# Two orders changed in the weight and attention prologue: w2's tiles go between the blocks of w3 @ w_out, and the last early pair makes its x before what the next pair needs

## The chip, the cores and the metric

The kernel runs on one core of one Trainium2 chip. The metric is device time in microseconds (us) of one execution. Three executions of the kernel before took 998.71, 1000.65 and 995.85 us; their median is 998.71 us. A further execution was profiled; it took 999.64 us, and its span from the first to the last instruction is 997.8 us.

## The reference

Block-causal attention over 8 batches of 8 heads (576 positions, head dimension 64), whose output is the input x of a gated MLP without a nonlinearity. In short:

```python
scores = scale * q @ k.T            # masked: a block of 64 sees itself and earlier blocks
attn   = exp(scores - max) ; attn /= attn.sum(-1) + 1e-9
x      = (attn @ v)                 # 4608 tokens x 512
out    = ((x @ w1) * (x @ w2) @ w3) @ w_out
```

## The kernel before, in words

Attention goes by pairs of heads: pair n holds heads 2(n mod 4) and 2(n mod 4)+1 of batch n div 4, 32 pairs in all, four pairs to a batch. Within a pair, j = 0, 1 is the head. The MLP goes by batch and by half of the tokens. Products are of float32r halves: a value is kept as a high part (`w1h`, `xh`) and the small rest (`w1l`, `xl`), and three products stand for one.

There are two phases. In the **early phase** (pairs 0 to 3, the whole of batch 0) the weights are made ready beside the attention. The weights come from memory as int64 views of doubles; `load_w` (L122) fetches one tile of 512 KB (`wraw`, five buffers) through the SP queue, ACT takes an absolute value (L137), and DVE puts the bits together in three operations (L138, L139, L142). For tiles of w1 and w2 `load_split` (L146) adds an ACT cast to the high part (L148) and a DVE subtraction for the rest (L149). w3 and w_out are multiplied together first: eight blocks `w` of eight products each (L359), copied out on ACT (L347) and DVE (L348) into `wh` and `wl`. The generator `gen_w` (L337) sets that order: 8 tiles of w_out, then for each of the 8 blocks two tiles of w3 and one tile of w1 (`rows1`), and behind them the 8 tiles of w2: 40 steps, one for each letter C of the plan.

A pair is written out by a string of letters, one string for each j. S is a tile of scores (`s_tile`, L223: two products for each part, then the exponentials on ACT). V is a step of scores @ v (tile `x`, L270 early, L286 late). M is a step of `shift_mask` for the **next** pair (L162): bf16 casts `kb` and `qd` on ACT, six groups of products `mx` (L180), their maxima `m` on DVE (L184, L186), a transpose on PE (`mt`, L188), a scaled copy on ACT (`ms`, L190), and two small transfers that put the row into `qk` of each j (L197). A and B are the halves of q and k for the next pair's j = 0 and this pair's j = 1 (L205, L207, L208). N takes `x` out of PSUM (`tr`, L310; L312), T divides by the sums and makes `xh` and `xl` (`norm` L320, `finish_x` L326). Q prepares v and loads the raw q, k and v of the pair after next (L94).

In the early phase a scheduler orders each engine's instructions once, when the program is built; all steps but C have the higher priority there. From pair 4 on (the **late phase**) PE's order is the written one: the scores of pair 4 (`s`, L231) come first, then the first products of the MLP (`ab`, L382), which read `xh` and `xl` of all four pairs of batch 0. Each engine works its list in order. The early tiles and the late tiles share memory.

The names and lines that matter below: `ms` and `qk` (L190, L197), `s` (L231), `x`, `rr`, `rb`, `xh`, `xl` (L310 to L334), `wraw`, `wbits`, `w2h`, `w2l` (L132 to L149), `kb`, `qd` (L158), `mx`, `m`, `mt` (L180 to L188), `ab` (L382). In the changed kernel the same statements stand 7 or 8 lines lower (`s` is L238 there, `ab` L390).

Of the kernel before, what the change touches and what calls it, by code (L numbers as in the profile page):

```python
# [17 lines left out]
B, H, S, D = 8, 8, 576, 64  # L18
BLK = 64
NB = S // BLK  # L20
NPAIR = H // 2
# [3 lines left out]
NC = DM // P  # L25
# [17 lines left out]
PLAN = (  # L43
    "B F B F S F S B F F S S F F F S M M V F V V V F R F F V Q N",
    "M A S S A F F S F M M S F F F S M A M V V V F V F F V N Q F R T M F F",
)

EARLY_PLAN = (
    "M S S S C S C C C C M S V V B C M M V A V M V M Q B M A B M N",
    "S C C S A S S C S C V V V V V Q N T",  # L50
)

DELAY = 3
# [5 lines left out]
def block_causal_attention__then__gated_mlp_kernel(ctx, tc, qkv, consts, ident_in, w1, w2, w3t, wout, out_t):  # L59
    nc = tc.nc  # L60
    w1, w2, w3t, wout = (w.bitcast(I32) for w in (w1, w2, w3t, wout))
# [12 lines left out]
    w1h = cpool.tile([P, NC, DF], F32R, name="w1h")  # L74
    w1l = cpool.tile([P, NC, DF], F32R, name="w1l")
# [7 lines left out]
    w2h = cpool.tile([P, NC, DF], F32R, name="w2h")  # L83
    w2l = cpool.tile([P, NC, DF], F32R, name="w2l")
# [37 lines left out]
    def load_w(dst, src, k):  # L122

        t = tl["early"].tile([P, 1024], F32, tag="wraw", name="wraw", bufs=5)
        u = tl["early"].tile([P, 512], F32, tag="wbits", name="wbits", bufs=6)  # L130
        wide = t.bitcast(I32)
        nc.sync.dma_start(out=wide.rearrange("p (k w) -> p k w", k=k), in_=src)  # L132
        wide = wide.rearrange("p (c two) -> p c two", two=2)
        low, high = wide[:, :, 0], wide[:, :, 1]
        bits = u.bitcast(I32)
        V = nc.vector
        nc.scalar.activation(u, high.bitcast(F32), AF.Abs, scale=2.0**-112)  # L137
        V.tensor_scalar(out=bits, in0=bits, scalar1=3, scalar2=0x7FFFFFF8, op0=ALU.logical_shift_left, op1=ALU.bitwise_and)  # L138
        V.scalar_tensor_tensor(out=bits, in0=high, scalar=-0x80000000, in1=bits, op0=ALU.bitwise_and, op1=ALU.bitwise_or)  # L139
        if dst is None:  # L140
            dst = u.unsqueeze(1)
        V.scalar_tensor_tensor(out=dst.bitcast(I32), in0=low.rearrange("p (k w) -> p k w", k=k), scalar=29,  # L142
                               in1=bits.rearrange("p (k w) -> p k w", k=k), op0=ALU.logical_shift_right, op1=ALU.bitwise_or)
        return u

    def load_split(dst_h, dst_l, src):  # L146
        val = load_w(None, src.unsqueeze(1), 1)
        nc.scalar.copy(dst_h, val)  # L148
        nc.vector.tensor_tensor(out=dst_l, in0=val, in1=dst_h, op=ALU.subtract)  # L149

    def load_rows(dst_h, dst_l, src, c):
        for h in range(2):
            cs = slice(h * 512, (h + 1) * 512)
            load_split(dst_h[:, c, cs], dst_l[:, c, cs], src[c * P : (c + 1) * P, h * 1024 : (h + 1) * 1024])
            yield
# [43 lines left out]
    def prep_qk(n, j):  # L199
        rqk = raw_of[n][:, 0 : 2 * S].rearrange("p (t s) -> p t s", t=2)  # L200
        o, x = own[j], oth[j]
        if j == 1:
            shift(n, 1)
        high, low = qk[j][o, 0::3, :], qk[j][o, 1:3, :]
        cast(n, high, rqk[o], CAST[0])  # L205
        yield
        nc.sync.dma_start(out=qk[j][x, 0::2, :].bitcast(F32), in_=high.bitcast(F32))  # L207
        (nc.vector if n <= EARLY else nc.gpsimd).tensor_tensor(out=low, in0=rqk[o], in1=high, op=ALU.subtract)  # L208
        yield
# [86 lines left out]
    def sums(n, j, part):  # L296

        blocks = tl["sum"].rearrange("p (b c) -> p b c", c=32)
        nc.vector.tensor_reduce(part[:, j, :], blocks, axis=AX.X, op=ALU.add, apply_transpose=True)
# [7 lines left out]
    def take_early(n, j, xps, x32, rr):  # L307
        o, x = own[j], oth[j]
        tr = work.tile([P, S], F32, tag="tr", name=f"tr{n}_{j}")
        nc.vector.transpose(tr[o], xps[x, 384:960])  # L310
        nc.vector.tensor_scalar_add(rr[o], tr[o].rearrange("p (b c) -> p b c", c=32)[:, :, 0], 1e-9)
        nc.scalar.copy(x32[o], xps[o, 384:960])  # L312
# [24 lines left out]
    def gen_w(wp):  # L337
        wo = tl["wo"]
        for k in range(NF):
            load_w(wo[:, k : k + 1, :], wout[k * P : (k + 1) * P, :].unsqueeze(1), 1)  # L340
            yield
        rows1 = (None for c in range(NC) for _ in load_rows(w1h, w1l, w1, c))
        pending = []

        def evacuate():
            m, acc = pending.pop(0)
            nc.scalar.copy(wh[:, m, :], acc)  # L347
            nc.vector.tensor_tensor(out=wl[:, m, :], in0=acc, in1=wh[:, m, :], op=ALU.subtract)  # L348

        for m in range(NF):  # L350
            t3 = wp.tile([P, NF, P], F32, tag="w3", name="w3", bufs=2)
            for k in range(0, NF, 4):
                src = w3t[k * P : (k + 4) * P, 2 * m * P : 2 * (m + 1) * P].rearrange("(k p) f -> p k f", p=P)
                load_w(t3[:, k : k + 4, :], src, 4)
                if k == 0:
                    yield
            acc = ps_m.tile([P, 512], F32, tag="psm", name=f"w{m}")
            for k in range(NF):
                nc.tensor.matmul(acc, t3[:, k, :], wo[:, k, :], start=(k == 0), stop=(k == NF - 1))  # L359
            pending.append((m, acc))  # L360
            if len(pending) > 1:
                evacuate()
            yield
            next(rows1)
            yield
        while pending:
            evacuate()
        for c in range(NC):
            yield from load_rows(w2h, w2l, w2, c)

    def gen_moe(b):
        mp, gh, gl = tl["late"], tl["gh"], tl["gl"]
# [33 lines left out]
    def fill(g, k):  # L406
        for _ in range(k):
            if next(g, "end") == "end":
                return
# [7 lines left out]
    for j in range(2):  # L417
        prep_v(0, j)
    load(1)
    weights = gen_w(wp)  # L420

    def pair(n):

        early = n < EARLY
        x32 = work.tile([P, S], F32, tag="x32", name=f"x32_{n}")
        rr = work.tile([P, S // 32], F32, tag="rr", name=f"rr{n}")
        part = None if early else work.tile([P, 2, S // 32], F32, tag="part", name=f"part{n}")
        last = n + 1 == NN
        masks = iter(()) if last else shift_mask(n + 1)
        own_qk = prep_qk(n, 1)  # L430
        next_qk = iter(()) if last else prep_qk(n + 1, 0)
        for j in range(2):
            xps = ps_x.tile([P, 1024], F32, tag="psx", name=f"x{n}_{j}")
            p_early = wp.tile([P, 1600], F32, tag="pe", name=f"pe{n}_{j}") if early else None
            tiles = iter(S_TILES)
            pvs = (pv_early if early else pv)(n, j, xps, p_early)
            delay = DELAY if n == NPAIR and j == 0 else 0
            for step in (EARLY_PLAN if early else PLAN)[j].split():
                if step == "C":
                    fill(weights, 1)  # L440
                    continue
                with tc.high_priority(offset=0) if early else nullcontext():
                    if step == "S":
                        s_tile(n, j, next(tiles), p_early)
                    elif step == "F":
                        if delay:
                            delay -= 1
                        else:
                            fill(mlp, 1)
                    elif step == "M":  # L450
                        fill(masks, 1)
                    elif step == "A":
                        fill(next_qk, 1)
                    elif step == "B":
                        fill(own_qk, 1)
                    elif step == "V":
                        fill(pvs, 1)
                    elif step == "R":
                        sums(n, j, part)
                    elif step == "N" and early:  # L460
                        take_early(n, j, xps, x32, rr)
                    elif step == "N":
                        take(n, j, xps, x32)
                    elif step == "T":
                        if not early:
                            total(n, part, rr)
                        norm(n, x32, rr)
                        finish_x(n, x32)
                    elif step == "Q" and not last:
                        if n + 1 != NPAIR:  # L470
                            prep_v(n + 1, j)
                        if j == 1 and n + 2 < NN:
                            load(n + 2)
# [64 lines left out]
```

## Time and profile before

| | |
|---|---|
| three runs, us | 998.71, 1000.65, 995.85 |
| median, us | 998.71 |
| profiled execution: time / span, us | 999.64 / 997.8 |
| instructions in the trace | 18149 |
| busy share of the span: PE, DVE, ACT, POOL | 96%, 71%, 55%, 52% |
| mean granted TensorE clock | 0.989 |

Shares over the whole span mix three stages: the early phase (to about 148 us), the late phase with attention and MLP together (to about 950 us), and the last MLP alone. The page's 40 slices show DVE at 7 to 9 tenths in the first six slices and PE at 9 tenths from then on; the slices of POOL are 0 up to there. So the rows further down are by stage: busy time of each engine in a stretch, who waited for whom in it, and the single instructions around the hand-over from the early to the late phase.

### The profile page before, as it was taken

Reading aid. Unit: us, or ns where it says so; the run is one execution under the profiler, and the core shown is the slowest. Engines: PE = TensorE matmul, PEld = TensorE weight load, DVE = VectorE, ACT = ScalarE, POOL = GpSimd, SP = SyncE. Lnnn points to the kernel's source line nnn. Section 1 sums busy time; section 2 is a strip of 40 time slices with the busy share of each in tenths; the row PEclk is TensorE's granted clock in tenths of the full one; section 3 lists DMA queues with packets and bytes.
Section 4 is the critical chain, followed back from the end, with each engine's and each line's share of the span. In section 5 each row is a group of like instructions: output and inputs, shape, how many; then the busy total and the mean of one; then the engine's idle time right before and its main releaser. Section 6 shows DMA issues by size and latency. Waiting matters only on the chain.

```text
span 997.8 us, 18149 instructions
## 1 busy us (share of the span) xinstructions
PE 959.7 (96%) x6624; PEld 884.9 (89%) x6624; DVE 705.7 (71%) x1316; ACT 546.5 (55%) x1433; POOL 520.3 (52%) x525
## 2 busy tenths in 40 slices
PE   3799979999999999999999999999999999999998
PEld 2455459999999999999999999999999999999998
DVE  7889987777777777777777777777777777774100
ACT  4556765555555656555556556555555555554221
POOL 0000007666666657676666756666665757573211
PEclk9799989999999999999999999999999999999999
DMA  7777521221222122212212221221221222100000
GB/s 235 232 254 239 184 94 35 64 73 56 79 62 86 58 77 62 64 47 74 72 57 79 62 86 50 86 61 47 64 74 62 68 79 62 45 17 26 3 23 24
DMA packets 36409, 80.39 MB, mean 81 GB/s; under 512 B 4384, under 2 KB 20896, under 8 KB 36320
## 3 DMA queue, kind: packets, MB, share of 16 engines
q1 hardware_dynamic: 36320, 79.23, 26.5%
q8 instruction: 52, 0.85, 0.4%
q14 instruction: 37, 0.30, 0.1%
HBM read 50.76 MB, written 9.44 MB: 60 GB/s over the span
## 4 chain that ended last, share of the span: by engine, by line
PE 69%; DVE 17%; ACT 7%; issue 4%; DMA 2%; DVEq 0%; ACTq 0%; SPq 0%
PE ab L382 28%; PE o L398 21%; PE s L231 7%; DVE pl L249 6%; PE x L286 5%; PE mx L180 3%; PE w L359 3%; ACT p L246 2%; DVE g L389 2%; ACT ph L247 2%; PE x L270 2%; DVE m L184 1%; DMA wraw<-in_w 1%; DVE x L324 1%; ACT a L387 1%
## 5 line engine op out<-in xcount | busy, mean ns | idle before, releaser
L252 POOL TENSOR_TENSOR rsum<-rsum,p 128x448 f32<-128x448 f32 x224 | 177.9, 794 | 120.7 <-ACT p L246 114.0
L249 DVE TENSOR_TENSOR pl<-p,ph 128x448 fp32r<-128x448 f32 x168 | 150.8, 911 | 65.0 <-ACT ph L247 64.2
L390 ACT CAST gh<-g 128x288 fp32r<-128x288 f32 x128 | 55.4, 433 | 218.1 <-DVE g L389 218.1
L391 POOL TENSOR_TENSOR gl<-g,gh 128x288 fp32r<-128x288 f32 x128 | 108.2, 845 | 122.6 <-ACT gh L390 122.5
L231 PE MATMUL s<-qk 128*128 128x288 f32 (+4 forms) x768 | 159.5, 315 | 5.0 <-DMA qk<-ms 2.2
L382 PE MATMUL ab<-xh,w1h 128*128 128x288 f32 x512 | 151.9, 297 | 3.5 <-ACT xh L333 3.5
L382 PE MATMUL ab<-xh,w2h 128*128 128x288 f32 x512 | 153.9, 301 | 0.0
L398 PE MATMUL o<-gh,wh 128*128 128x288 f32 x512 | 153.5, 300 | 0.0
L382 PE MATMUL ab<-xl,w1h 128*128 128x288 f32 x512 | 151.6, 296 | 0.0
L382 PE MATMUL ab<-xh,w1l 128*128 128x288 f32 x512 | 151.6, 296 | 0.0
L382 PE MATMUL ab<-xl,w2h 128*128 128x288 f32 x512 | 151.1, 295 | 0.0
L382 PE MATMUL ab<-xh,w2l 128*128 128x288 f32 x512 | 151.1, 295 | 0.0
L398 PE MATMUL o<-gh,wl 128*128 128x288 f32 x512 | 150.9, 295 | 0.0
L398 PE MATMUL o<-gl,wh 128*128 128x288 f32 x512 | 150.9, 295 | 0.0
L208 POOL TENSOR_TENSOR qk<-raw,qk 64x1152 fp32r<-64x1152 f32 x54 | 144.2, 2671 | 2.0
L184 DVE TENSOR_REDUCE m<-mx 128x1 f32<-128x512 f32 (+6 forms) x320 | 128.6, 449 | 20.7 <-PE mx L180 18.9
L221 POOL TENSOR_TENSOR vs<-raw,vs 128x320 fp32r<-128x320 f32 x56 | 49.6, 887 | 166.5 <-ACT vs L158 166.5
L231 PEld LDWEIGHTS s<-qk 128*128 128x128 f32 (+1 forms) x768 | 116.8, 184 | 19.1 <-issue 7.0
L247 ACT ACTIVATE ph<-s 128x288 fp32r<-128x288 f32 x336 | 131.3, 393 | 0.0
L246 ACT ACTIVATE p<-s 128x448 f32<-128x448 f32 x224 | 85.4, 381 | 45.3 <-PE s L231 44.2
L389 DVE TENSOR_TENSOR g<-ab,a 128x288 f32<-128x288 f32 x128 | 57.7, 451 | 73.6 <-PE ab L382 70.4
L286 PE MATMUL x<-ph,vs 128*128 128x128 f32 x336 | 104.1, 319 | 0.0
(70 smaller groups left out, 2134.1 us busy)
## 6 DMA issues: line engine op xcount, KB each, us to landing
raw<-in_qkv SPq DMA_DIRECT2D x32, 896.0 KB
qk<-qk SPq DMA_DIRECT2D x64, 288.0 KB
out_t<-o SPq DMA_DIRECT2D x64, 144.0 KB
wraw<-in_w3t SPq DMA_DIRECT2D x16, 512.0 KB
wraw<-in_w SPq DMA_DIRECT2D x16, 512.0 KB
wraw<-in_wout SPq DMA_DIRECT2D x8, 512.0 KB
qk<-ms SPq DMA_DIRECT2D x64, 2.2 KB
cst<-in_consts SPq DMA_DIRECT2D x1, 288.0 KB
```

Source lines behind the costliest of these rows:

```text
L184: nc.vector.reduce_max(m[:, col : col + 1], sc, axis=AX.X)
L208: (nc.vector if n <= EARLY else nc.gpsimd).tensor_tensor(out=low, in0=rqk[o], in1=high, op=ALU.subtract)
L231: nc.tensor.matmul(t[ks, at : at + q1 - q0], qk[j][:, 2 + s, kr], qk[j][:, s, q0:q1], start=(s == 0), stop=(s == 1))
L246: nc.scalar.activation(p32, t[ks, at : at + w], AF.Exp, scale=SCALE)
L247: nc.scalar.activation(ph[ks, o : o + w], t[ks, at : at + w], AF.Exp, scale=SCALE)
L249: nc.vector.tensor_tensor(out=low, in0=p32, in1=ph[ks, o : o + w], op=ALU.subtract)
L252: nc.gpsimd.tensor_tensor(out=r, in0=r, in1=p32, op=ALU.add)
L286: nc.tensor.matmul(xps[:, to : to + w], v[:, c, :], pr[:, a : a + w], start=(u < 2 and s == 0), stop=(u in (0, len(PV) - 1) and s == len(p ...
L382: nc.tensor.matmul(t[:, 0:HALF], l[:, c, fs], r, start=(c == 0 and s == 0), stop=(c == NC - 1 and s == 2))
L389: nc.vector.tensor_tensor(out=g32, in0=acc[1][:, 0:HALF], in1=a32, op=ALU.mult)
L391: nc.gpsimd.tensor_tensor(out=gl[:, f, :], in0=g32, in1=gh[:, f, :], op=ALU.subtract)
L398: nc.tensor.matmul(t[:, 0:HALF], l[:, f, es], r[:, f, :], start=(f == 0 and s == 0), stop=(f == NF - 1 and s == 2))
```

## The change

Two things change. In `gen_w` one list of tiles holds w1's eight and then w2's eight, and `ROWS` says how many of them follow each block of w3 @ w_out: 1, 1, 2, 2, 2, 2, 2, 2. Fourteen go between the blocks, and two remain for the end. In the last early pair (pair 3) the plan is `LAST_PLAN`: no M and no A before the T that finishes x; then nine M and four A, which belong to pair 4. The first three early pairs keep their plan.

```diff
+ROWS = (1, 1, 2, 2, 2, 2, 2, 2)
+
+LAST_PLAN = (
+    "S S S S C C S V V B B V V V Q C C C C C N",
+    "S S S S S V V V V V C C C C C N T Q M M M M M M M M M A A A A",
+)
...
-        rows1 = (None for c in range(NC) for _ in load_rows(w1h, w1l, w1, c))
+        rows = (None for d in ((w1h, w1l, w1), (w2h, w2l, w2)) for c in range(NC) for _ in load_rows(*d, c))
...
-            next(rows1)
-            yield
+            for _ in range(ROWS[m]):
+                next(rows)
+                yield
         while pending:
             evacuate()
-        for c in range(NC):
-            yield from load_rows(w2h, w2l, w2, c)
+        for _ in rows:
+            yield
...
-            for step in (EARLY_PLAN if early else PLAN)[j].split():
+            for step in (PLAN if not early else LAST_PLAN if n + 1 == NPAIR else EARLY_PLAN)[j].split():
```

On DVE, the end of the early phase before. `tr`, `rr`, `rb`, `x_3` and `xl` are pair 3's x; `m_932` is the maxima for pair 4, `qk_85` its q and k of j = 1, `pl` pair 4's exponentials.

```order
L186 TENSOR_REDUCE m_932<-m_932 128x1
L139 SCALAR_TENSOR_TENSOR wbits<-wraw,wbits 128x512
L138 TENSOR_SCALAR wbits<-wbits 128x512
...
L310 STREAM_TRANSPOSE tr_1_1067<-x_1_998 64x576
...
L208 TENSOR_TENSOR qk_85<-raw_834,qk_85 64x1152
L149 TENSOR_TENSOR w2l<-wbits,w2h 128x512
...
L324 TENSOR_TENSOR x_3_852<-x_3_852,rb_1072 128x576
L249 TENSOR_TENSOR pl<-rsum,ph 128x288 x2
L334 TENSOR_TENSOR xl_0_1076<-x_3_852,xh_0_1075 128x288
L334 TENSOR_TENSOR xl_1_1080<-x_3_852,xh_1_1079 128x288
```

The same place on DVE now (`m_1047` are the maxima for pair 4):

```order
L156 TENSOR_TENSOR w2l<-wbits,w2h 128x512
L317 STREAM_TRANSPOSE tr_1_1025<-x_1_965 64x576
L191 TENSOR_REDUCE m_1047<-mx_0_1048 128x1
...
L331 TENSOR_TENSOR x_3_845<-x_3_845,rb_1030 128x576
L191 TENSOR_REDUCE m_1047<-mx_4_1064 128x1
L191 TENSOR_REDUCE m_1047<-mx_2_1054 128x1
L191 TENSOR_REDUCE m_1047<-mx_4_1064 128x1
L341 TENSOR_TENSOR xl_0_1034<-x_3_845,xh_0_1033 128x288
L191 TENSOR_REDUCE m_1047<-mx_5_1069 128x1 x2
L341 TENSOR_TENSOR xl_1_1038<-x_3_845,xh_1_1037 128x288
L193 TENSOR_REDUCE m_1047<-m_1047 128x1
L215 TENSOR_TENSOR qk_85<-raw_827,qk_85 64x1152
L256 TENSOR_TENSOR pl<-rsum,ph 128x288 x2
```

The last tile of w2 and the whole of x now stand before the last maximum of pair 4; before, the maxima were done first, and x came last.

On PE, the hand-over before: the scores' first product, the transpose of the maxima, the other scores, and the MLP.

```order
L270 MATMUL x_1_998<-pe_1_999,ve_144 128x64
L231 MATMUL s_0_1108<-qk_84 128x288
L188 MATMUL mt_989<-ident,m_932 9x128
L231 MATMUL s_0_1108<-qk_84 128x288
L231 MATMUL s_0_1114<-qk_84 128x288 x2
L382 MATMUL ab<-xh_0_353,w1h 128x288
```

And now:

```order
L277 MATMUL x_1_965<-pe_1_966,ve_144 128x64
L238 MATMUL s_0_1108<-qk_84 128x288
L187 LDWEIGHTS qd
L187 MATMUL mx_3_1059<-kb_1043,qd 128x384
...
L187 LDWEIGHTS qd
L187 MATMUL mx_5_1069<-kb_1043,qd 128x64
L195 MATMUL mt_1075<-ident,m_1047 9x128
L238 MATMUL s_0_1108<-qk_84 128x288
L238 MATMUL s_0_1114<-qk_84 128x288 x2
L390 MATMUL ab<-xh_0_353,w1h 128x288
```

Groups 3 to 5 of `mx` moved behind the last product of pair 3's x; the order from `mt` on is as it was.

On SP, the transfers at the end of the early phase before (`raw_1065` is pair 5's q, k and v):

```order
L132 DMA wraw<-in_w 128x1024 x2
L197 DMA qk_85<-ms_752 1x9x64
L207 DMA qk_85<-qk_85 64x2x576
L132 DMA wraw<-in_w 128x1024
L94 DMA raw_1065<-in_qkv 128x1792
L207 DMA qk_84<-qk_84 64x2x576
```

And now (`raw_1041` is the same data):

```order
L139 DMA wraw<-in_w3t 128x4x256 x2
L139 DMA wraw<-in_w 128x1024
L101 DMA raw_1041<-in_qkv 128x1792
L139 DMA wraw<-in_w 128x1024 x3
L214 DMA qk_84<-qk_84 64x2x576
```

The raw load of pair 5 moved ahead of the last three tiles of w2.

## Rows read from the trace of the kernel before

**Rows 1.** Stretches: length, busy us of each engine, clock, DMA share, GB/s

```profile
65.00:148.00 83.00, 74.12 (x265) 41.77 (x264) 80.63 (x156) 55.73 (x112) 2.37 (x2) 0.97 0.59 186
148.00:950.00 802.00, 797.12 (x5902) 775.53 (x5902) 570.53 (x1058) 448.76 (x1237) 509.61 (x508) 1.00 0.21 61
```

**Rows 2.** PE in order of time: start, us, instruction [idle before]

```profile
135.20 0.52 PE L180 MATMUL mx<-kb,qd 128*128 128x320 bf16 x4
...
137.94 0.27 PE L188 MATMUL mt<-ident,m 128*9 128x128 f32 x1
140.41 1.09 PE L231 MATMUL s<-qk 128*128 128x288 f32 x3 [2.19 <-DMA qk<-ms]
141.29 0.44 PE L382 MATMUL ab<-xh,w1h 128*128 128x288 f32 x1
...
143.21 0.44 PE L382 MATMUL ab<-xl,w1h 128*128 128x288 f32 x1
147.11 0.61 PE L382 MATMUL ab<-xh,w1h 128*128 128x288 f32 x1 [3.46 <-ACT xh L333]
...
148.10 1.48 PE L231 MATMUL s<-qk 128*128 128x448 f32 x4
```

**Rows 3.** DVE's waits, 65 to 148 us

```profile
DVE tr L310 <- PE x L270: 0.7, 1, 0.7
```

**Rows 4.** DVE in order of time

```profile
52.89 0.69 DVE L184 TENSOR_REDUCE m<-mx 128x1 f32<-128x512 f32 x1 [2.23 <-PE mx L180]
...
135.73 1.22 DVE L184 TENSOR_REDUCE m<-mx 128x1 f32<-128x320 f32 x4 [0.57 <-PE mx L180]
...
137.59 0.15 DVE L186 TENSOR_REDUCE m<-m 128x1 f32<-128x2 f32 x1
137.66 0.68 DVE L139 SCALAR_TENSOR_TENSOR wbits<-wraw,wbits 128x512 int32<-128x512 int32 x1
138.26 0.42 DVE L138 TENSOR_SCALAR wbits<-wbits 128x512 int32<-128x512 int32 x1
138.59 0.69 DVE L142 SCALAR_TENSOR_TENSOR wbits<-wraw,wbits 128x512 int32<-128x512 int32 x1
...
139.91 0.78 DVE L310 STREAM_TRANSPOSE tr<-x 64x576 f32<-64x576 f32 x1
...
142.14 1.35 DVE L208 TENSOR_TENSOR qk<-raw,qk 64x1152 fp32r<-64x1152 f32 x1
...
146.46 0.82 DVE L249 TENSOR_TENSOR pl<-rsum,ph 128x288 fp32r<-128x288 f32 x2
147.19 0.82 DVE L334 TENSOR_TENSOR xl<-x,xh 128x288 fp32r<-128x288 f32 x2
```

**Rows 5.** ACT in order of time

```profile
135.76 0.67 ACT L158 CAST kb<-raw 128x576 bf16<-128x576 f32 x1 [0.18 <-PE mx L180]
136.34 0.61 ACT L148 CAST w2h<-wbits 128x512 fp32r<-128x512 f32 x1
136.86 1.35 ACT L158 CAST qd<-raw 64x576 bf16<-64x576 f32 x2
138.25 0.27 ACT L190 ACTIVATE ms<-mt 9x128 fp32r<-9x128 f32 x1
```

**Rows 6.** Stretches of the hand-over, columns as in Rows 1

```profile
140.00:143.60 3.60, 3.19 (x12) 2.90 (x12) 3.51 (x6) 2.16 (x5) 0.49 (x1) 0.53 0.01 1
...
147.10:150.30 3.20, 3.19 (x11) 3.02 (x12) 1.11 (x4) 1.90 (x6) 0.59 (x1) 0.50 0.62 255
```

**Rows 7.** SP's issues: start, us; the second a late w2 tile's

```profile
95.25 7.94 SPq L132 DMA_DIRECT2D wraw<-in_w  x5
...
118.33 0.52 SPq L132 DMA_DIRECT2D wraw<-in_w  x1
```

**Rows 8.** That late tile's first use, on ACT

```profile
122.47 0.67 ACT L137 ACTIVATE wbits<-wraw 128x512 f32<-128x512 f32 x1 [0.18 <-DMA wraw<-in_w]
```

**Rows 9.** Chain that ended last: start, us, one transfer of a w tile

```profile
96.78 6.12 DMA wraw<-in_w
```

## The prediction

> **What bounds the kernel now.** I read the busy time of each engine by stretches first [rows 1]. From 148 to 950 us PE is busy for 797.12 of 802.00 us at full clock: whatever the early phase ends late or early by is handed through to the end, since there is no slack of PE in which it could be caught up. From 65 to 148 us it is DVE that is full, 80.63 of 83.00 us; PE's 74.12 there are products waiting in its pipeline. So the question is when the early phase hands over. Next I read PE's instructions around the hand-over in order of time, with what ended each idle stretch [rows 2]. Two waits count: 2.19 us of the scores `s` for the row of maxima that a transfer puts into `qk`, and 3.46 us of `ab` for `xh`, pair 3's x. The reader is to see that PE has finished `mt` at 138.21 and stands until 140.41, does three products of `s` and nine of `ab` to 143.65, stands until 147.11, and then never again: at 148.10 come the next scores, and the late phase runs. The second wait is the one that the new order of pair 3 takes away, for x is then finished before the masks of pair 4. What it puts last instead is the row of maxima.
>
> **The first part, w2's tiles earlier.** On DVE no instruction is added or taken away; the early list holds the same operations in another order. Up to about 69 us the list is also in the same order. From there to the hand-over DVE had no more than two real waits, 0.7 us for `x` [rows 3] and 0.57 for `mx` [rows 4], 1.3 us together. A better order can save at most these, a worse one can add some; the longest wait that DVE had for another engine earlier is 2.23 us [rows 4]. Both ends kept, I take half of the 1.3 as saved, 0.65 us. w2 ready earlier is worth nothing by itself: its first use is behind `s` and twelve `ab`. `wh` and `wl`, now ready later, are wanted only by the second MLP stage. Both are covered by the work of the late phase.
>
> **The second part, x first, step by step.** *When DVE is through.* Before, its last early work, `xl`, ends at 147.19 + 0.82 = 148.01; the two `pl` between 146.46 and 147.19 belong to pair 4 and take 0.73 [rows 4]. Without them the early work ends at 147.28, with 0.65 saved at 146.6. In the new order the last early operation is `qk_85` (L215), so 146.6 is its end; the bounds are 146.0 (1.3 saved) and 148.8 (2.23 added).
>
> *When the row of maxima is there.* Counted back from that end: `qk_85` 1.35, the small reduction 0.07 from start to start, two `xl` of 0.37 each, and the maxima of 192, 256 and 64 columns. Four maxima of 832 columns in all went in 1.22 [rows 4], so these 512 columns are some 0.7. That makes 2.85: at 143.75 the PSUM buffer of the last mask group comes free. Its two products follow, some 0.4 (four took 0.52 [rows 2]), to 144.15. Then ACT: `ms` stands behind `kb` and both `qd` of pair 5, which may start only when those products have read `kb` and `qd`. Before, `kb` started at 135.76 and `ms` at 138.25, with one `w2h` of 0.52 from start to start between them that is not there any more [rows 5]: 2.49 - 0.52 = 1.97. So `ms` starts at 146.1. (By the other way, through the last reduction and `mt`, it could start at 146.6 - 1.35 + 0.5 = 145.75, where 0.5 is from the end of L186 to `ms` [rows 4, 5]; ACT's casts are later and decide.) From the start of `ms` to the first `s` after the transfer it was 140.41 - 138.25 = 2.16 [rows 2, 5]. So PE starts at 146.1 + 2.16 = 148.3. Behind that wait on PE stands everything: the other scores and all of `ab`, though x is ready some 3 us earlier. That is what is late next.
>
> *What PE then has to do.* Before, it had done three `s` and nine `ab` while x was on its way, and had three `ab` left. Now three `s` and all twelve `ab` lie between the wait and the next scores. At the low clock three `s` took 0.88 and one `ab` 0.24 ((143.21 - 141.29) / 8) [rows 2]: 0.88 + 2.88 = 3.76. The next scores would be at 152.1, against 148.10.
>
> *The clock.* After its wait for x, PE ran at 0.50 of full clock, level 1.2 GHz, from 147.1 to 150.3, and at full clock in the stage that follows; behind the first wait it was 0.53 over 3.6 us [rows 1, 6]. In the new order there is one long stand, and before it PE has only masks and the rest of x. I take the same 3.2 us of low clock, 148.3 to 151.5. Then the last 0.56 us of the 3.76 take half, and the next scores start at 151.8: 3.7 us later than before. At that point the kernel before still had 2.2 us of low clock ahead, which cost it 1.1; the new one has none. Sum: 3.7 - 1.1 = 2.6 us slower. The bounds: with 146.0 and full clock at once the 3.76 shrink to 1.88, the point comes at 149.6, and the sum is 149.6 - 148.1 - 1.1 = 0.4; with 148.8 and a low clock as long as both stretches of before together, 6.8 us, it is 2.6 + 2.2 + 1.8 = 6.6. I take 2.6, since both stands of before were followed by a low clock of about that length.
>
> The Trainium skill, page "TensorE: Matmul & The Clock Gate", section "HAM oscillation — how this bites in real kernels", says that a pause in the products is paid twice, once as the pause and again as throttled products after it. Rows 6 show that here behind both pauses. By that rule the sum is 2.6; without it, with full clock at once, it would be 3.76 / 2 + 148.3 - 148.1 - 1.1 = 1.0.
>
> Against the profiled execution that is 999.64 + 2.6 = 1002.2 us. That execution lay 0.93 over the median of the three runs; by the median it is 998.71 + 2.6 = 1001.3 us, which I forecast.
>
> **Rivals.** *The gain is what it looks like.* If the row of maxima were there before PE needs it, the 3.46 us of wait for x and the low clock behind it (3.2 / 2 = 1.6) would go: 999.64 - 5.1 = 994.5, by the median 993.6. For it speaks that the wait for x is the longest of PE at the hand-over [rows 2]. Against it stands the order: no `ab` comes before the second `s`, and the last maximum is the last but one of DVE's early operations. Chance 0.05.
>
> *Even.* The new wait is as long as the old, with full clock soon behind it: the sum of the lower bound, 0.4, to 1.0: 999.1 to 999.7 by the median. For it speaks that the maxima wait and the x wait hang on the same full DVE. Chance 0.22.
>
> *A wait on the last w2 tile, slower.* On SP the raw load of pair 5 now stands before the last three tiles. The last tile may be asked for when the fifth tile before it has been read, and between that and its own first DVE operation stand ten operations of DVE: six of 0.60 from start to start, two of 0.33, a transpose of 0.78 [rows 4] and a small one of some 0.1, 5.1 us, less 0.67 for ACT's step [rows 8]: 4.4 us for the transfer. A tile of the end of the phase took 122.47 - 118.33 = 4.14 [rows 7, 8], and fits; one of five that were issued from 95.25 on took 6.12 [rows 7, 9], and DVE would stand 1.7 us. From 4.4 us of transfer on this decides; with it nothing of DVE's 1.3 is saved either, and the sum is 2.6 + 1.7 + 0.65 = 5.0, by the median 1003.7 and more if two tiles are late. Chance 0.25 for this and all else that is over 5 us.
>
> The Trainium skill, page "DMA: Bandwidth & Descriptors", section "Anatomy of one DMA — SWDGE (gpsimd) path", gives a transfer as 2.0 us and a share by size; for 512 KB that is 3.2 us, an estimate by that page for another issuing path. Rows 7 and 8 show 4.14, and the measurement decides. By the page the last tile would have 1.2 us to spare, and this rival would fall.
>
> *The change doesn't do what it says* is excluded by the order: x does come before the maxima, w2 before the last block.
>
> **Chances and range.** Forecast (1 to 5 us slower) 0.48, even 0.22, slower by over 5 us 0.25, faster 0.05. What a measurement here can tell from no change is 0.5%, about 5 us. So faster 0.05, same 0.70, slower 0.25. The bounds are 0.4 and 6.6 over the median, 999.1 to 1005.3; the three runs lie 2.9 below to 1.9 above theirs, so I widen by about 1 to 1.5 us: 997.8 to 1006.0.
>
> **What would show it.** In the changed kernel's trace: DVE full from 65 us to its last `qk_85` at 146 to 147.3, with no wait for a `wraw` tile; PE's wait for `xh` gone; in its place a wait of `s` for the transfer `qk<-ms` that ends at about 148.3; then a low clock for some 3 us; the scores of 448 columns at about 151.8, and everything later shifted by the same 2.6 us. I am wrong if `s` starts much before 147, if PE finds other work while it waits, if a `wraw` tile holds ACT's L144 and so DVE, or if the clock stays high through the stand.

## The result and the profile after

The changed kernel takes 1003.2 us (median of 8 runs, 1000.76 to 1006.52), the kernel before 998.04 us beside it (8 runs): a ratio of 1.005, 95% interval 1.0032 to 1.0067. The forecast was 1001.3, its range 997.8 to 1006.0. The profiled execution of the changed kernel took 1002.75 us, with a span of 1000.5.

The two profiled executions can't be laid on each other by their starts. On DVE both kernels have the same list up to a `qk` subtraction and a little past it; before, it stands at 65.13, after at 63.50:

```profile
65.13 1.34 DVE L208 TENSOR_TENSOR qk<-raw,qk 64x1152 fp32r<-64x1152 f32 x1
```

```profile
63.50 1.34 DVE L215 TENSOR_TENSOR qk<-raw,qk 64x1152 fp32r<-64x1152 f32 x1
```

The profiled execution of before lost 1.63 us ahead of it, at a granted clock of 0.89 from 0 to 65 us, where after had 0.95. So I count from this mark. A second mark is the last p @ v of pair 4's first head (`x<-ph`, 128x64), called head 1 below. The two stretches, before first (columns as in [rows 1]):

```profile
65.13:157.45 92.32, 83.44 (x325) 50.96 (x324) 86.83 (x165) 59.16 (x123) 8.69 (x8) 0.96 0.56 176
```

```profile
63.50:160.69 97.19, 83.45 (x322) 50.41 (x324) 86.48 (x165) 59.23 (x123) 7.53 (x8) 0.93 0.54 168
```

The reader is to see that PE, the second column, works for 83.4 us in both, and that the stretch is 4.87 us longer, about the 5.2 between the medians. The idle times ahead of PE's instructions in it that the view prints sum to 8.70 us before and 13.67 after: 4.97 more. That is the whole loss: PE stands longer, that is, it is idle and waits. And since its busy time is the same in both, the granted clock, 0.96 and 0.93 in the mean, is not what makes the difference.

PE after, against [rows 2]:

```profile
139.57 0.59 PE L187 MATMUL mx<-kb,qd 128*128 128x384 bf16 x2 [1.73 <-DVE m L191]
142.49 0.58 PE L187 MATMUL mx<-kb,qd 128*128 128x320 bf16 x2 [2.33 <-DVE m L191]
...
145.31 0.38 PE L195 MATMUL mt<-ident,m 128*9 128x128 f32 x1 [1.10 <-DVE m L193]
148.36 1.09 PE L238 MATMUL s<-qk 128*128 128x288 f32 x3 [2.67 <-DMA qk<-ms]
149.25 0.44 PE L390 MATMUL ab<-xh,w1h 128*128 128x288 f32 x1
...
151.89 0.44 PE L390 MATMUL ab<-xl,w1h 128*128 128x288 f32 x1
152.13 0.92 PE L238 MATMUL s<-qk 128*128 128x448 f32 x4
```

The wait of `ab` for `xh` is gone. In its place PE stands before `mx` for the PSUM buffers that DVE's maxima free, and then before `s` for the row of maxima. Three `s` and twelve `ab` lie behind that wait. ACT after, against [rows 5]:

```profile
144.25 0.67 ACT L165 CAST kb<-raw 128x576 bf16<-128x576 f32 x1 [0.33 <-PE mx L187]
144.83 1.35 ACT L165 CAST qd<-raw 64x576 bf16<-64x576 f32 x2
146.20 0.27 ACT L197 ACTIVATE ms<-mt 9x128 fp32r<-9x128 f32 x1
```

The hand-over by stretches, against [rows 6]; the clock is the third figure from the end:

```profile
145.70:148.30 2.60, 0.00 (x0) 0.00 (x0) 0.95 (x1) 0.74 (x2) 0.00 (x0) 0.50 0.01 1
148.30:152.50 4.20, 4.14 (x17) 4.12 (x18) 0.92 (x2) 1.45 (x5) 0.00 (x0) 0.53 0.64 219
152.50:160.00 7.50, 7.50 (x55) 7.23 (x55) 5.85 (x8) 3.27 (x11) 5.17 (x6) 1.00 0.18 39
```

DVE after, against [rows 3, 4]: its largest wait, and its last early work.

```profile
129.57 0.69 DVE L156 TENSOR_TENSOR w2l<-wbits,w2h 128x512 fp32r<-128x512 f32 x1 [1.83 <-ACT w2h L155]
...
144.75 0.45 DVE L341 TENSOR_TENSOR xl<-x,xh 128x288 fp32r<-128x288 f32 x1
145.11 0.15 DVE L193 TENSOR_REDUCE m<-m 128x1 f32<-128x2 f32 x1
145.29 1.36 DVE L215 TENSOR_TENSOR qk<-raw,qk 64x1152 fp32r<-64x1152 f32 x1
```

What ACT did ahead of that wait, and what SP had issued, against [rows 7, 8]:

```profile
128.36 0.67 ACT L144 ACTIVATE wbits<-wraw 128x512 f32<-128x512 f32 x1 [2.49 <-DMA wraw<-in_w]
128.93 0.60 ACT L155 CAST w2h<-wbits 128x512 fp32r<-128x512 f32 x1
```

```profile
113.96 0.34 SPq L101 DMA_DIRECT2D raw<-in_qkv  x1
122.32 0.33 SPq L139 DMA_DIRECT2D wraw<-in_w  x1
```

The raw load of pair 5 stands ahead of the last three w2 tiles on SP. The tile that ACT waits 2.49 us for is the last of them: issued at 122.32, first used at 128.36, 6.04 us later. The cast `w2h` is of an earlier tile, whose own input was ready; it stands behind that wait in ACT's list, and DVE waits for it.

### The profile page after: what moved, and what is told of

It is laid out like the page before. It is cut to its first block, busy times and chain, and to the rows that moved or that the text cites. A ratio compares the mean times of both kernels' runs of the same rounds, so it can differ in the third digit from the quotient of the medians.

```text
span 1000.5 us, 18121 instructions
## 1 busy us (share of the span) xinstructions
PE 958.2 (96%) x6594; PEld 883.3 (88%) x6624; DVE 705.2 (70%) x1316; ACT 546.6 (55%) x1433; POOL 519.3 (52%) x525
## 4 chain that ended last, share of the span: by engine, by line
PE 66%; DVE 18%; ACT 9%; issue 4%; DMA 2%; DVEq 0%; ACTq 0%; SPq 0%
PE ab L390 28%; PE o L406 21%; PE s L238 7%; DVE pl L256 6%; PE x L293 5%; PE mx L187 3%; DVE g L397 2%; ACT p L253 2%; ACT ph L254 2%; PE w L366 2%; DVE m L191 1%; DMA wraw<-in_w 1%; PE x L277 1%; DVE wbits L146 1%; DVE x L331 1%
## 5 line engine op out<-in xcount | busy, mean ns | idle before, releaser
L238 PE MATMUL s<-qk 128*128 128x288 f32 (+4 forms) x768 | 156.8, 312 | 7.7 <-ACT pe L246 3.3
L191 DVE TENSOR_REDUCE m<-mx 128x1 f32<-128x512 f32 (+5 forms) x320 | 128.7, 449 | 20.5 <-PE mx L187 17.4
L238 PEld LDWEIGHTS s<-qk 128*128 128x128 f32 (+1 forms) x768 | 115.8, 183 | 20.4 <-ACT pe L246 6.7
```

Source lines behind the costliest of these rows:

```text
L191: nc.vector.reduce_max(m[:, col : col + 1], sc, axis=AX.X)
L238: nc.tensor.matmul(t[ks, at : at + q1 - q0], qk[j][:, 2 + s, kr], qk[j][:, s, q0:q1], start=(s == 0), stop=(s == 1))
```

## The experiments

All were timed in 5 rounds beside the kernel before, whose medians were 997.6 to 998.1. This table gives the main instants in us from the DVE mark: the end of `xl`, the end of the last `qk` of early work, the start of `ms`, of the scores of 448 columns, and the last p @ v of pair 4's first and second head. `stands` is PE's idle time from the mark to the first of these two; in e4_warm products that nobody reads fill a part of it. Line numbers (L238) can be a few higher or lower in a kernel than in the changed one.

| kernel | `xl` | `qk` | `ms` | scores | head 1 | head 2 | stands | ratio, 95% interval |
|---|---|---|---|---|---|---|---|---|
| before | 82.88 | 78.36 | 73.12 | 82.97 | 92.32 | 103.74 | 8.70 | |
| after | 81.70 | 83.15 | 82.70 | 88.63 | 97.19 | 108.60 | 13.67 | 1.005, 1.0032 to 1.0067 |
| e1_rows | 82.15 | 78.65 | 72.87 | 82.24 | 91.91 | 103.33 | 7.88 | 0.9997, 0.9984 to 1.001 |
| e2_plan | 81.85 | 83.30 | 82.85 | 88.68 | 97.19 | 108.61 | 12.26 | 1.0033, 1.0022 to 1.0045 |
| e3_rawlate | 80.15 | 81.60 | 81.09 | 87.02 | 96.09 | 107.49 | 12.47 | 1.0042, 1.0027 to 1.0057 |
| e4_warm | 81.31 | 82.75 | 82.33 | 87.49 | 96.43 | 107.84 | 8.60 | 1.0033, 1.0021 to 1.0045 |
| e5_mlpfirst | 83.68 | 85.13 | 85.14 | 92.04 | 100.08 | 115.08 | 13.36 | 1.0093, 1.0081 to 1.0106 |
| e6_lead2_rawlate | 80.16 | 81.60 | 81.93 | 86.98 | 94.73 | 105.14 | 10.15 | 1.0061, 1.0048 to 1.0074 |
| e6b_lead4_rawlate | 83.41 | 84.87 | 85.07 | 90.13 | 98.43 | 109.52 | 10.30 | 1.0088, 1.0074 to 1.0103 |
| e7_before_mlpfirst | 82.11 | 77.09 | 73.32 | 86.34 | 94.56 | 109.42 | 11.24 | 1.0066, 1.0054 to 1.0078 |
| e8_before_delay5 | 82.54 | 78.03 | 72.79 | 78.71 | 91.93 | 104.87 | 10.41 | 0.995, 0.9936 to 0.9963 |
| e9_after_delay5 | 81.45 | 82.91 | 82.46 | 86.03 | 95.75 | 107.17 | 13.85 | 0.9982, 0.9968 to 0.9995 |
| e10_fill_gaps | 81.00 | 82.44 | 82.54 | 89.40 | 97.93 | 109.56 | 11.96 | 1.0098, 1.0081 to 1.0115 |
| e11_rows_delay5 | 83.80 | 78.42 | 72.65 | 77.32 | 89.06 | 100.47 | 6.95 | 0.9938, 0.9924 to 0.9953 |

**One part alone: e1_rows.** `LAST_PLAN` is not used, w2's tiles stay between the blocks.

```diff
-            for step in (PLAN if not early else LAST_PLAN if n + 1 == NPAIR else EARLY_PLAN)[j].split():
+            for step in (EARLY_PLAN if early else PLAN)[j].split():
```

> Only w2's tiles between the w3 blocks; all four early pairs keep the old plan. Theory (the slowdown is made by the last pair's order: its hand-over, about 3 us, and a raw load put ahead of the last w2 tiles, about 2 us): here the masks of pair 4 come before x again, and on SP the raw load of pair 5 stands behind all tiles, so 998 us, ratio 1.000, within 0.002; PE waits for xh again by some 3 us, and DVE has no wait of over 1 us from 65 us on. Rival (w2's tiles between the blocks cost by themselves, because the w3 blocks end later and w2's tiles hold DVE up): 1001 to 1003 us, ratio 1.003 to 1.005, and DVE waits for w2h before the hand-over.

Measured 998.24 us. The first part costs nothing. PE's waits are the two of before, 3.2 and 2.6 in place of 2.19 and 3.46 [rows 2]:

```profile
PE s L238 <- DMA qk<-ms: 3.2, 1, 3.2
PE ab L390 <- ACT xh L340: 2.6, 1, 2.6
```

Here, too, ACT waits for the last w2 tile, and longer than in the changed kernel; but with the old plan DVE has other work in its list meanwhile, and no wait of over 0.2 us from 120 us on:

```profile
127.31 0.68 ACT L144 ACTIVATE wbits<-wraw 128x512 f32<-128x512 f32 x1 [3.15 <-DMA wraw<-in_w]
```

**The other part alone: e2_plan.**

```diff
-ROWS = (1, 1, 2, 2, 2, 2, 2, 2)
+ROWS = (1, 1, 1, 1, 1, 1, 1, 1)
```

> Only the new plan of the last early pair; w2's tiles come last as before. Theory: the hand-over keeps its new order (s waits for the row of maxima, three s and twelve ab lie behind that wait), which costs some 3 us; the raw load is behind all tiles on SP, so the 2 us of DVE's waits for late w2 tiles are gone: 1001 us, ratio 1.003. Rival (the two parts only cost together, or the plan alone is harmless): 998 us, ratio 1.000. Rival (the plan is the whole of it): 1003 us, ratio 1.005.

Measured 1001.61 us. By the trace the second part alone makes the whole loss: head 1 comes at 97.19, as in the changed kernel. By the medians it makes 3.8 of 5.2 us, and the two intervals overlap. I had expected DVE's waits of the changed kernel to be gone with w2 back at the end. They are as long, only in other places:

```profile
DVE tr L317 <- PE x L277: 1.8, 3, 1.2
DVE w1l L156 <- ACT w1h L155: 1.3, 1, 1.3
```

Here the wait for `w1h` has the same form as the one for `w2h` in the changed kernel, at another w2 tile: ACT waits for the tile, and the ready cast stands behind it.

```profile
106.47 0.67 ACT L144 ACTIVATE wbits<-wraw 128x512 f32<-128x512 f32 x1 [2.26 <-DMA wraw<-in_w]
```

From the mark to the end of its early work DVE waits 1.43 us in before and 1.25 in e1, with the old plan, and 3.11 in e2 and 3.17 in the changed kernel, with the new one: the plan makes these waits, and the order of w2's tiles does not. ACT waited for a tile of w before as well, 2.07 us at 102.92 as its longest from 95 us on, and DVE did not stand for it. That DVE runs dry for want of the masks, which the new plan takes out of pair 3's first head, is how I read this; no run shows it by itself.

**The raw load behind the last w2 tiles: e3_rawlate.** A copy of one element makes pair 5's raw load wait for a late w2 tile.

```diff
         t = raws.tile([P, RAW], F32, tag="raw", name=f"raw{n}")
+        if n == NPAIR + 1:
+            nc.gpsimd.tensor_copy(t[0:1, 0:1], w2h[0:1, 2, 0:1].bitcast(F32))
         nc.sync.dma_start(out=t, in_=qkv[n // NPAIR, n % NPAIR])
```

> The changed kernel with one edit: a one-element POOL copy makes the raw load of pair 5 wait for a cast of w2, so that on SP it stands behind the last four w2 tiles. Theory: DVE's wait of 1.83 us for w2h at 129.6 us goes (ACT no longer stands in front of a late tile), the early phase ends some 1.8 us earlier, and the time is 1001.3 us, ratio to the kernel before 1.003 where the changed kernel has 1.005. Rival (the tile is late for another reason, such as its buffer coming free late): the wait stays at over 1 us, and the time at 1003 us.

Measured 1002.07 us. The wait falls from 1.83 to 0.67:

```profile
126.97 0.69 DVE L158 TENSOR_TENSOR w2l<-wbits,w2h 128x512 fp32r<-128x512 f32 x1 [0.67 <-ACT w2h L157]
```

DVE's early work ends 1.55 us earlier than in the changed kernel (81.60 against 83.15), and of that 1.10 arrives at head 1. The medians, 1002.07 and 1003.2 with intervals that overlap, don't tell it apart.

**The clock: e4_warm.** 24 unread products of 512 columns fill PE's gaps up to `mt`.

```diff
+                if warm and s == 1:
+                    d = ps_m.tile([P, 512], F32, tag="psm", name="warm")
+                    for _ in range(WARM):
+                        nc.tensor.matmul(d, wh[:, 0, 0:P], wh[:, 0, :], start=True, stop=True)
```

> The changed kernel with 24 further products of 512 columns on PE, whose results nobody reads; they stand in PE's list in the gaps between the mask groups at the hand-over, up to mt. Theory (the low clock behind the long stand costs some 2 us of the slowdown): the granted clock stays at 1.00 through the gaps, twelve ab behind the wait take 1.6 us where they took 2.9, and the time is 1.5 to 2 us under the changed kernel's, 1001.5 us, ratio 1.0035; if the extra products hold up the masks, some tenths of that are lost. Rival (the low clock is hidden by other waits of the late phase's start, on ACT or DVE): 1003 us, as the changed kernel.

Measured 1001.56 us. In the stretches the clock is 1.00 up to 148.3, and 0.59 behind the 2.8 us in which PE stands for `s`:

```profile
130.00:148.30 18.30, 12.10 (x56) 8.32 (x57) 15.48 (x29) 9.87 (x21) 1.71 (x2) 1.00 0.08 17
148.30:152.50 4.20, 4.20 (x21) 4.11 (x20) 0.98 (x3) 2.37 (x7) 0.45 (x1) 0.59 0.64 218
```

So filling the gaps ahead only moved the low clock, and brought 0.76 us at head 1. The time that I had expected came, 1.6 us under the changed kernel, but not by the way that I had expected, and the intervals of the two overlap. The low clock behind the stand is still there, so e4 does not show what that one costs; that the clock is not the loss is read from PE's busy time above. The Trainium skill, page "TensorE: Matmul & The Clock Gate", section "HAM oscillation — how this bites in real kernels", has a pause paid for twice, as the pause and as throttled products behind it; the trace agrees, with 2.8 us of one stand and 0.59 behind it.

**MLP products into the gaps: e5 to e7.** x is ready before the row of maxima, so the first steps of the MLP went ahead of pair 4's scores, and the three left-out steps (`DELAY`) went to later places of the pair. e6 and e6b (1002.93 and 1006.61 us) have e3's late raw load and two and four steps more; e7 is the edit of e5 on the kernel before.

```diff
+LEAD = 0                         # e6: 2, e6b: 4
+SKIP = (8, 12, 14)               # e6: and 18, 21; e6b: and 6, 10, 18, 21
...
+            if n == NPAIR and j == 0:
+                fill(mlp, LEAD)
...
-                        if delay:
-                            delay -= 1
-                        else:
+                        seen.append(step)
+                        if n != NPAIR or len(seen) not in SKIP:
                             fill(mlp, 1)
```

> The changed kernel with one thing moved: the first twelve products of the MLP (ab, which need x of the four early pairs and not pair 4's row of maxima) stand ahead of pair 4's scores instead of behind them; the three places at which the MLP skips a step come later in pair 4, so that the number of steps is the same. Theory (what the change costs at the hand-over is the order behind the wait for the row of maxima: 3 s and 12 ab at low clock stand behind it): nine of the twelve ab fall into PE's gaps before the wait, at most some four products stay behind it, the next scores come 2 to 3 us earlier than in the changed kernel, counted from the first common DVE marker, and the time is 1000.3, ratio to before 1.002; DVE's own 1.8 us of waits stay, so it does not reach before. Rival (DVE's end alone sets the time, the products behind the wait are hidden anyway): 1002.5 to 1003, ratio 1.005. Rival (clock): the products in the gaps keep the clock high, and 1 us more is gained: 999.

> The changed kernel with the late raw load of e3 (it stands behind the last tiles of w2) and two more steps of the MLP, 24 ab instead of 12, ahead of pair 4's scores; five places instead of three at which the MLP skips a step, later in pair 4. Theory: the wait for the row of maxima is then filled with products that have to be done anyway, PE has 12 ab (1.45 us at full clock, 2.9 at low) less ahead of it than with twelve, and DVE ends some 1 us earlier: 997 to 998.6, ratio 0.999 to 1.001, so the x-first order is as good as before or a little better. Rival (filling the wait only makes pair 4's softmax, which ACT has to do, later, so nothing but e5's gain comes): 1000 or more. Rival (the evacuation of ab runs into DVE's full stretch and delays the row of maxima itself): 1002 or more, with a wait of s longer than 2.7 us.

> As e6, with 36 more ab in place of 12 (four steps of the MLP ahead of pair 4's scores, seven skips later). Theory: the wait of PE before s is some 2.7 us plus what the twelve ab in the gaps leave; two more steps are enough to fill it, so four put some 1 to 1.5 us of products in front of scores that could run: 997.5 to 999.5, not better than e6. If the early late phase is PE's bound alone, and it does not matter which products come first, e6 and e6b are the same within 0.1%.

> The kernel before with the same edit as e5: the first twelve ab ahead of pair 4's scores. Theory: in the old order x of pair 3 is last (PE stands 3.46 us for it), so the three products that need it hold the scores, which could have run: 998.0 to 1000, ratio 1.000 to 1.002. Rival (the edit is a gain by itself, whatever is last): 995.5 to 996.5, ratio 0.998.

Measured 1007.49, 1002.93, 1006.61 and 1004.14 us: all four missed. The edit did two things at once. In e5 the twelve `ab` between the scores stayed behind the wait and others came ahead of it; and where steps were now left out, PE stood. Its waits from 150 to 200 us in e5, of which before and after have only the kind of the last line, 0.3 us once:

```profile
PE s L239 <- ACT ph L255: 1.5, 1, 1.5
PE ab L391 <- DVE g L398: 0.7, 1, 0.7
PE x L294 <- DVE ph L257: 0.6, 1, 0.6
PE x L294 <- DVE pl L257: 0.6, 2, 0.3
```

In e7 the three `ab` that need pair 3's x stand ahead of the scores, and PE stands eight us in one piece:

```profile
146.15 0.61 PE L383 MATMUL ab<-xh,w1h 128*128 128x288 f32 x1 [8.00 <-ACT xh L334]
```

They show that the MLP's steps in pair 4 cover waits for ACT and DVE, and nothing of the cause. e6 shows a little more: at head 2 it is 2.35 us ahead of e3 (105.14 against 107.49), and then `tot`, PE's product for the sums, waits 2.3 us for DVE and the gain is spent.

**Five left-out steps in place of three: e8, e9, and as the reverse e10.** Here one thing changes: the scores of 448 and 320 columns stand ahead of the first `ab`, and twelve `ab` come later.

```diff
-DELAY = 3
+DELAY = 5
```

> The kernel before with five instead of three MLP steps left out at the start of pair 4 (they come later, the products are the same in all): the scores of 448 and 320 columns now stand ahead of the first ab that need pair 3's x. Theory (after the runs so far: the number of PE's products is fixed, so what counts is how long PE stands in all, 8.7 us from the common DVE marker to the first p @ v of pair 4's end in the kernel before): the wait of 3.46 us for x is filled with some 1.5 us of scores, so PE stands 1 to 1.5 us less and the time is 996 to 997, ratio 0.998 to 0.999. Rival (the ab that stood between the scores were the cover for ACT's exponentials, and PE stands as long for these as it saves): 997.5 to 998.5, ratio 1.000.

> The changed kernel with the same edit: behind the wait for the row of maxima stand three s and then at once the next scores, the twelve ab come later. Theory (PE's standing time counts): the wait in front of s is not filled by this, the twelve products are only done later, and PE stands some 0.8 us more for the exponentials that the ab covered: 1001 to 1003, ratio 1.004, the next scores after s 1.5 to 2.5 us earlier and nothing of it in the end. Rival (my sum's term: the twelve ab behind the wait, 2.88 us at low clock, are themselves the price): 1000 to 1000.5, ratio 1.002.

> The changed kernel with the late raw load of e3, no MLP step left out in pair 4 (so that twelve ab can go into PE's gaps ahead of s, and six more follow the first scores), and in their place one step left out at the very end of each of the pairs 5, 6 and 7, so that the number of steps up to the end of the batch is the same. Theory (standing time counts): PE's gaps before s take some 1.5 us of products that have to be done anyway, as in e6, while pair 4's exponentials keep their cover: PE stands 1 to 1.5 us less than in e3 and the time is 1000 to 1001, ratio 1.002 to 1.003, still over before, whose PE stands some 2.5 us less. Rival (the steps left out at the ends of pairs 5 to 7 were cover as well): PE stands up to 0.8 us more at each, 1002 to 1003, and the trace shows waits there that the changed kernel has not.

Measured 993.04, 995.67 and 1007.61 us, all three outside what either theory had. At the hand-over e9 did what was expected: the scores come 2.60 us earlier than in the changed kernel, head 1 and head 2 1.44 and 1.43, and twelve products of 0.132 us each, 1.58 us, are still to be done. Nothing is gained there, so the twelve `ab` behind the wait are not the price. In e8 the wait for x was not turned into a gain either: PE stands 10.41 in place of 8.70 us, 2.8 of them for ACT's `ph` and 2.4 for DVE's `g`.

The time came from a place that neither theory had named: all later pairs. From pair 4's head 2 to the last pair's it is 743.62 us in the changed kernel (172.10 to 915.72) and 736.61 in e9 (170.37 to 906.98), with the same products: 0.26 less for each of 27 pairs. In 200 to 880 us, the changed kernel first, then e8 and e9:

```profile
200.00:880.00 680.00, 675.67 (x4984) 656.79 (x5008) 503.12 (x932) 393.68 (x1085) 447.68 (x444) 1.00 0.23 66
```

```profile
200.00:880.00 680.00, 678.92 (x5019) 660.67 (x5043) 504.15 (x944) 400.26 (x1093) 470.19 (x448) 1.00 0.23 66
```

```profile
200.00:880.00 680.00, 679.49 (x5027) 661.68 (x5052) 505.09 (x945) 400.31 (x1093) 468.45 (x449) 1.00 0.23 66
```

PE is 3.8 us busier in e9 than in the changed kernel. The changed kernel has twelve waits in this stretch, the kernel before the same, and e9 none:

```profile
PE x L293 <- DVE pl L256: 3.5, 12, 0.3
```

DVE's `pl` came 0.3 us too late for the p @ v products; two steps of the MLP later, it no longer does. The other 3 us are no wait in the trace; a hint is that the products `x<-pl` take 354 ns in the median there and 310 in e8 and e9.

e10 has e3's late raw load, `DELAY = 0`, and this:

```diff
-                        if delay:
-                            delay -= 1
-                        else:
+                        seen += 1
+                        if not (NPAIR < n < 2 * NPAIR and j == 1 and seen in HOLES):
                             fill(mlp, 1)
```

(`HOLES` is the last step of the head.) The small waits for `pl` stay, 3.8 us from 160 us to the end, and a new one comes that I had not expected at that place, pair 5's second score:

```profile
180.89 0.40 PE L241 MATMUL s<-qk 128*128 128x288 f32 x1 [3.12 <-DMA qk<-ms]
```

There `ms` started at 175.52, so the small transfer took up to 5.4 us to its first use in place of 2.2. SP's list has a likely reason: pair 7's raw load, 896 KB, was issued just ahead of the row of maxima. In the changed kernel it comes behind it (175.73 against 174.03).

```profile
176.31 0.33 SPq L104 DMA_DIRECT2D raw<-in_qkv  x1
176.73 0.79 SPq L207 DMA_DIRECT2D qk<-ms  x1
```

No run has put the two the other way round in e10, so this is not shown.

**The first part with five left-out steps: e11_rows_delay5**, is e1_rows with the number changed:

```diff
-DELAY = 3
+DELAY = 5
```

> The first part of the change alone (w2's tiles between the blocks) on the kernel before, with five MLP steps left out at the start of pair 4 as in e8. Theory (w2's order is worth nothing either way, as in e1; five left-out steps take away the small waits of x for pl in every later pair): the same as e8, 993 us, ratio 0.995, no wait of x for pl from 200 us on, and PE over 99.8 of 100 us there. Rival (the gain of e8 hangs on how pair 4 happens to begin): 996 to 998 with the waits of 0.3 us back.

Measured 991.55 us, ratio 0.9938, interval 0.9924 to 0.9953: faster than both kernels, not told apart from e8 (the intervals overlap), and what I would keep. The same stretch, 200 to 880 us:

```profile
200.00:880.00 680.00, 679.47 (x5029) 661.72 (x5053) 506.96 (x950) 400.43 (x1094) 471.80 (x451) 1.00 0.23 65
```

Beside it e9, the whole change with the same edit, is 4.1 us slower (995.67), with before at 997.94 and 998.11 beside them, and their ratios' intervals don't meet. With three left-out steps the same difference, after against e1, is 5.0. So the second part costs about the same with either number. The row of e11 in the table is of its fastest execution, 988.37, and shows more of a difference than the medians.

## Why the prediction was right, and which term was off

The sign, the place and the way from DVE's end to the next scores were right; DVE's end was not, and the sum of 2.6 us was too small by half.

*What bounds it.* Right. From head 2 to the last instruction the kernel before takes 828.9 us and the changed one 828.4: what the early phase ends late by is handed through. What I did not see was the rest of slack in the late phase, the waits for `pl`.

*w2's tiles earlier are free.* Right by themselves (e1).

*DVE is through at 146.6.* The instant came out, 145.29 + 1.36 = 146.65, but by chance, since the profile of before had lost 1.63 us ahead of the mark. From the mark I had 146.6 - 65.13 = 81.47, and it was 83.15. This is the step that failed: I took half of DVE's 1.3 us of waits as saved, and they grew. From the mark to the end of its early work DVE waited 1.43 us before and 3.17 after, 1.7 more. Its value lay inside the bounds given (2.23 added), not at the one taken.

The forecast had named the sign: no wait for a `wraw` tile, and that I am wrong if one holds ACT's L144 and so DVE. One did. It is the event of the rival "a wait on the last w2 tile": the last tile took 6.04 us, where the rival had 6.12, and DVE stood 1.83, where it had 1.7. But e3 takes 1.16 of this wait away and gives back only 1.10 of the 4.87 us, and e2, whose last tile is not late, waits as long elsewhere. So the late tile is one way in which the waits happen. What is behind both is the new plan (e1 and e2 against before and after); that it does so by taking the masks, which had filled DVE, out of pair 3's first head is argued, and no run has put them back one by one.

*The row of maxima.* Right: `ms` starts 0.45 us ahead of the end of `qk` (forecast 0.5), held by `kb` and both `qd`, and `s` follows 2.16 after it (forecast 2.16).

*What PE then has to do, and the clock.* The next scores start 3.77 us after `s`, forecast 3.5, since the low clock lasted through all of it and not 3.2 us. What the kernel before still lost behind that point was 9.35 - 8.56 = 0.79 us (scores to head 1), not 1.1. The terms again: 2.6 + 1.68 + 0.27 + 0.31 = 4.86, against the 4.87 measured. As book-keeping the term holds; as a cause the products behind the wait do not (e9). The price is that PE stands 4.97 us longer ahead of them.

*The rivals.* "Even" and "the gain is what it looks like" are out. The third came nearer than the forecast: its time was 1003.7, mine 1001.3, and the measured one is 1003.2, so the loss of some 5 us lies on the border between the two. Its wait came, but its sum of 5.0 saw one tile as the cause, and e3 gives back 1.1 of the loss. That the time lies in the forecast's range is owed to the wide upper bound, and not to the terms taken.

## What to carry to other kernels

Of two results that a busy engine must make before a hand-over, try first the one with the longer way behind it: here the row of maxima needs a transpose, a copy and a transfer, 3.1 us from the last reduction (145.26 after) to the first score, while x needs none of these. And look whether the new order leaves work between the waits: DVE stood for late tiles only where the plan had moved its other work to the end. Count the change in how long the bounding engine stands between two marks that both traces share, not from the start of a profile. And where one engine is full for hundreds of us, ask for its small repeated waits: two steps of filler shifted took 0.26 us from each of 27 pairs, 7.0 us, more than the whole change cost.

## What the runs showed of the hardware that was not expected

In e4 the granted clock was 1.00 from 130 to 148.3 us, with a stand of PE of 2.8 us close to the end of it, and 0.59 over the next 4.2 us. The same small transfer of the row of maxima was in use 2.16 us after its copy on ACT began at the hand-over of before and after, and 5.4 us after in e10, where a raw load of 896 KB was issued just ahead of it. Tiles of 512 KB of w took 4.14 to 6.12 us [rows 7 to 9]; the last one in the changed kernel took 6.04 to its first use, and held ACT for 2.49.
